# A first strip of 576 tokens, and one batch's attention output made by token

## The chip, the cores and the metric

The kernel runs on one core of one Trainium2 chip. The metric is the device time of one execution in microseconds (us). The kernel before takes 312.56 us, the median of 3 runs (312.52 to 312.74). Smaller is better.

## The reference

Linear attention without a softmax, an RMS norm over each head's output, and a bilinear feed-forward layer, over 8 batches of 576 tokens (4608 tokens in all), 8 heads of 64:

```python
kv = np.einsum('bhsd,bhse->bhde', k, v)
out = np.einsum('bhsd,bhde->bhse', q, kv)
rms = np.sqrt(np.mean(out * out, axis=-1, keepdims=True) + 1e-06)
x = (out / rms * g_norm)          # then (b, s, h*d): 4608 x 512
a = x @ w_a                        # 512 -> 1536
b = x @ w_b
return (a * b @ w_out)             # 1536 -> 512
```

The inputs are float32; the kernel works in bfloat16 with float32 sums.

## The kernel before

**The feed-forward layer.** The 4608 tokens are cut into nine strips of 512 (`STRIP`). `xt` holds x transposed (features on the partitions, tokens along the row). For each strip, twelve units (`Unit`, called by `ffn_ab`, one for each 128 of the 1536 hidden features) make a and b: four matmuls with a weight block of `wa_t` (`part_a`), which ScalarE copies to SBUF, then four with `wb_t` (`part_b`), which VectorE multiplies by that copy into `abt`. Then four groups of 128 tokens (`ffn_o`, `o_mm`, `o_out`) multiply `abt` with `wo_t`: twelve matmuls each, a copy out of PSUM by VectorE or ScalarE in turn, and a store on SyncE's DMA queue (SP). Every one of these is a "product" (`product`, L159): a 128x128 weight block against 512 columns. While `halves[0]` is set, a product is issued as two matmuls of 64 weight columns each.

**Attention.** A batch has four pairs of heads. Its x can be made in two ways.
- By channel (batches 0 and 1): `qtr` transposes q on TensorE, `kv1` makes k'v, then x, the squares, their sums by a product with `ones` (`pss`, L227), the reciprocal root (L233) and the scaling into `xt` (`pst`, L240). Batch 1 uses `x` with the block-diagonal `kvb`.
- By token (batches 2 to 7): q is cast to bfloat16 into a DRAM tile `qs` by two GpSimd DMAs and transposed into `qT` by one DMA transpose on SP (`transpose_q`, L153). k and v are loaded into `ktl` and `vtl` by four GpSimd DMAs. `load_late` (L136) issues all six; its first instruction, the copy `gate`, holds GpSimd until the previous batch's `qT` has landed. `kv` (L170) makes k'v, `tx` (L286) x in five chunks c of 128 tokens (the last of 64 new ones), `tsq` squares on ScalarE, `tss` sums on VectorE, `trs` takes the root on ScalarE and multiplies by the gain on GpSimd (L330), and `txt` (L336) scales on VectorE into `x_tok` and issues a DMA transpose into `xt` on SP (L343).

**Order.** Every engine takes its instructions in the order in which the program writes them; there is no scheduler. Strip 0 runs on batch 0's x. Then strip 0's four groups of `ffn_o` are cut in `pieces` (L574), and between them stands batch 1's attention by channel. Then strips 1 to 7 run, and strip s has beside it the attention of batch s + 1: `slot(A, s, n)` (L601) is called after unit n, and once in the middle of it with n - 0.5, and a table says at which n stand `kv` (k0) and `tx` (x0) and how far after x0 each of the other steps stands. n = 12 to 15 are the strip's four groups of `ffn_o`. `load_late` and `transpose_q` of later batches stand at fixed n as well (L644 to L649).

**DMA queues.** GpSimd's queue brings, in this order: batch 0, the weights `wa_t` and `wb_t` in six column blocks of 256 (`load_ab`), the twelve rows of `wo_t`, batch 1's q, k and v, and then batch 2 (`load_late(2)`). SP's queue takes the stores and all DMA transposes, in program order: each waits there for what it reads.

Of the kernel before, what the change touches and what calls it, by code (L numbers as in the profile page):

```python
# [15 lines left out]
def kernel(  # L16
# [11 lines left out]
    nc = tc.nc  # L28
# [14 lines left out]
    EARLY = 2  # L43
    KORD = tuple(range(KC))

    pool = ctx.enter_context(tc.tile_pool(name="sb", bufs=1))
    psum = ctx.enter_context(tc.tile_pool(name="ps", bufs=1, space=bass.MemoryType.PSUM))

# [17 lines left out]

    qT = [sb([128, NP, S], BF16, f"qT{i}") for i in range(2)]
    kvs = [sb([128, NP, D], BF16, f"kvs{i}") for i in range(2)]

    kvb = sb([128, NP, 128], BF16, "kvb")  # L70
    xt = sb([128, KC, n_tok], BF16, "xt")
    abt = [[sb([128, STRIP], BF16, f"ab{i}_{f}") for f in range(FC)] for i in range(2)]
    a_sb = [sb([128, STRIP], BF16, f"asb{i}") for i in range(4)]
    sq = [sb([128, 2, HF], BF16, f"sq{i}") for i in range(3)]
    rs = [sb([128, 2, HF], FP32, f"rs{i}") for i in range(3)]
# [58 lines left out]
        nc.gpsimd.dma_start(out=wo_t[:, i, :], in_=wo_v[:, i, :])  # L134

    def load_late(b):  # L136
        if b > EARLY:

            nc.gpsimd.tensor_copy(gate, qT[(b - 1) % 2][0:1, 0, 0:1])  # L139
        d = qs_d[b].rearrange("t (h d) -> t h d", h=H)  # L140
        for hs in (slice(0, NP), slice(NP, H)):
            nc.gpsimd.dma_start(out=d[:, hs, :], in_=q[b, hs].rearrange("h t d -> t h d"))  # L142
        n = 128 * LC
        for t, src in ((ktl[b % 2], k), (vtl[b % 2], v)):
            nc.gpsimd.dma_start(  # L145
                out=t[:, :, 0:LC, :],
                in_=src[b, :, 0:n].rearrange("h (t c) d -> t h c d", c=LC),
            )
            nc.gpsimd.dma_start(
                out=t[0 : S - n, :, LC, :], in_=src[b, :, n:].rearrange("h t d -> t h d")  # L150
            )
# [12 lines left out]
    class Attn:  # L164
# [5 lines left out]
        def kv(self, p, o):  # L170
# [5 lines left out]
            for c, n in enumerate(rows):  # L176
                for j in range(2):
# [4 lines left out]
                        start=(c == 0),  # L182
                        stop=(c == len(rows) - 1),
                    )

        def kv_out(self, ps, src):
            for j in range(2):
                r = slice(j * D, (j + 1) * D)
                nc.scalar.copy(kvb[r, ps, r], src[r])


        def kv1(self, p, i):
# [57 lines left out]
                )  # L250


        def x(self, p, i0):
            for h in range(2):
                product(
                    P[:, i0 + h, 0:HF],
                    kvb[:, p, :],
                    self.qT[:, p, h * HF : (h + 1) * HF],
                    start=True,
                    stop=True,  # L260
                )

        def rows(self, c):
            t0 = min(c * 128, S - 128)
# [19 lines left out]
        def tx(self, lent):  # L286
            self.lent = lent
            for c in range(LC + 1):
                t0, _ = self.rows(c)
                for p in range(NP):  # L290
                    for j, (i, c0) in enumerate(self.place(c)):
                        r = slice(j * D, (j + 1) * D)
                        nc.tensor.matmul(  # L293
                            P[:, i, c0 + p * D : c0 + (p + 1) * D],
                            lhsT=self.qT[r, p, t0 : t0 + 128],
                            rhs=self.kvs[r, p, :],
                            start=True,
                            stop=True,
                        )


            _, r = self.rows(LC)
            for j, (i, _) in enumerate(self.place(LC)):
                nc.scalar.copy(
                    x_last[r, j], P[r, i, 0 : STRIP // 2].rearrange("t (p d) -> t p d", p=NP)
                )

        def tsq(self, c):
            _, r = self.rows(c)
# [7 lines left out]
                axis=mybir.AxisListType.X,  # L317
            )

        def trs(self, c):  # L320
            _, r = self.rows(c)
            n = r.stop - r.start
            nc.scalar.activation(  # L323
                rst[c % 3][r],
                sst[c % 3][r],
                AF.Abs_reciprocal_sqrt,
                bias=eps_t[r],
                scale=1.0 / D,
            )
            nc.gpsimd.tensor_mul(  # L330
                sqt[c % 3][r].rearrange("t j p d -> t (j p) d"),
                rst[c % 3][r].unsqueeze(2).to_broadcast([n, H, D]),
                g_all[r].unsqueeze(1).to_broadcast([n, H, D]),
            )
# [13 lines left out]
    class Unit:  # L348
        n = 0

        def __init__(self, s, fc, a, b):
            self.s, self.fc, self.a, self.b = s, fc, P[:, a, :], P[:, b, :]
            self.t = a_sb[Unit.n % 4]
            Unit.n += 1

        def mm(self, w, kcs):
            t0 = self.s * STRIP
            for kc in kcs:
                product(
                    self.a if w is wa_t else self.b,  # L360
                    w[:, kc, self.fc * 128 : (self.fc + 1) * 128],
                    xt[:, kc, t0 : t0 + STRIP],
                    start=(kc == KORD[0]),
                    stop=(kc == KORD[-1]),
                )
# [2 lines left out]
            self.mm(wa_t, kcs)  # L368
            self.mm(wb_t, kcs)

        def part_a(self, kcs=KORD):
            self.mm(wa_t, kcs)
            nc.scalar.copy(self.t, self.a)  # L373

        def part_b(self, kcs=KORD):
            self.mm(wb_t, kcs)
            nc.vector.tensor_mul(abt[self.s % 2][self.fc], self.b, self.t)  # L377

        def rest(self, kcs=KORD):
            self.part_a(kcs)  # L380
            self.part_b(kcs)

    ab_banks = [4, 1, 2, 0]

# [4 lines left out]
    def ffn_ab(s, fc, between=None):  # L389
        u = Unit(s, fc, ab_bank(), 0)  # L390
        u.part_a()
        if between:
            between()
        u.b = P[:, ab_bank(), :]
        u.part_b()

    def store(t0, t, e0, e1, eng=nc.sync):
# [14 lines left out]
    n_o = [0]  # L412

    def o_mm(s, g, i, fcs, e0=0, e1=d_model):
        for fc in fcs:
            product(
                P[:, i, e0:e1],
                abt[s % 2][fc][:, g * 128 : (g + 1) * 128],
                wo_t[:, fc, e0:e1],
                start=(fc == 0),  # L420
                stop=(fc == FC - 1),
            )
# [41 lines left out]
    make_identity(nc, ident, nomemset=True)  # L464
    nc.scalar.activation(warm, eps_t, AF.Abs_reciprocal_sqrt)
    nc.vector.memset(ones, 0.0)
    nc.vector.memset(kvb, 0.0)
    for t in ktl + vtl:
        nc.vector.memset(t[S - 128 * LC :, :, LC, :], 0.0)
    nc.vector.memset(ones[0:D, 0:D], 1.0 / D)  # L470
# [4 lines left out]
    for c in range(0, KC, 2):  # L475
        for w, src in ((wa_t, wa_v), (wb_t, wb_v)):
            nc.gpsimd.dma_start(out=w[:, c : c + 2, 0:WC], in_=src[:, c : c + 2, 0:WC])  # L477
    for i in range(1, d_ff // WC):
        load_ab(i * WC, (i + 1) * WC)
    for i in range(FC):  # L480
        load_o(i)
    for p in range(NP):
        load_pair(1, p)
    load_late(2)

    X, SS = (4, 0), 6

# [65 lines left out]
    u1.part_a((3,))  # L553
    u0.part_b((2, 3))
    u1.part_b((2, 3))

    u2 = Unit(0, 2, 0, 1)
    u3 = Unit(0, 3, 2, 0)
# [1 line left out]
    u3.part_a()  # L560
    u2.part_b()
    u3.part_b()
    for fc in range(4, FC):
        ffn_ab(0, fc)


    A = Attn(1)
    h1, h2 = range(0, FC // 2), range(FC // 2, FC)

    nc.sync.dma_start(out=gate_d, in_=vt[1][0:1, H - 1, EC - 1, D - 1 : D])  # L570
    nc.sync.dma_start(out=g_all, in_=g_norm.partition_broadcast(128))
    transpose_q(2)
    ffn_o(0, 0, X[0])
    pieces = [(1, h1), (1, h2), (2, h1), (2, h2), (3, h1), (3, h2)]  # L574
    for n, (g, fcs) in enumerate(pieces):

        halves[0] = n > 0
        o_mm(0, g, O, fcs)
        if fcs is h2:
            o_out(0, g, O)  # L580
        if 0 <= n - 2 < NP:
            A.pss(n - 2, SS)
            A.pst(n - 2, X[n % 2])
        if 0 <= n - 1 < NP:
            A.x(n - 1, X[(n - 1) % 2])
            A.psq(n - 1, X[(n - 1) % 2])
        if n < NP:
            A.qtr(n, 2)
            A.kv1(n, 2)
            A.kv_out(n, P[:, 2, STRIP - D :])  # L590
            A.qtr_out(n, 2)
    u0 = Unit(1, 0, 2, 3)
    u1 = Unit(1, 1, 4, 5)
    u0.first((0, 1, 2))
    u1.first((0, 1, 2))
    u0.rest((3,))
    u1.rest((3,))
    ab_banks[:] = [0, 1, 2]


    def slot(A, s, n):  # L601

        kb = P[:, 7, :].rearrange("q (b p e) -> q b p e", b=2, e=D)
        if s == 1:
            k0, xs = 5, (6.5, 8, 9.5, 11, 12.5)
        else:
            k0, x0 = {2: (2, 3.5), 3: (4, 5.5), 4: (0, 1.5), 5: (4, 5.5), 6: (0, 1.5)}[s]
            xs = tuple(x0 + x for x in (0, 1.5, 2.5, 4, 5))

        k0, x0 = {1: (5, 6.5), 2: (1, 2.5), 3: (4, 5.5), 4: (0, 0.5), 5: (4, 5.5), 6: (0, 0.5)}[s]  # L610
        if n == k0 and s in (1, 2, 3, 5):
            halves[0] = s < 5
            two = [A] if s < 3 else [A, Attn(s + 2)]
# [5 lines left out]
        m = n - x0  # L619
        if m == 0:  # L620
            A.tx(ab_bank())
        for c in range(LC + 1):
            if m == 1.5 * c:
                A.tsq(c)
            if m == (1, 2, 4, 5, 7)[c]:
                A.tss(c)
            if m == (1, 2, 4, 5, 7)[c] + 0.5:
                A.trs(c)
            if m == (1, 2, 4, 5, 7)[c] + 1.5:
                A.txt(c)  # L630

    for s in range(1, N_STRIP - 1):
        b = s + 1
        A = Attn(b) if b < B else None
        for n in range(FC + 4):
# [4 lines left out]
                ffn_ab(s, n, amid)  # L640
            if A:
                slot(A, s, n)

            if s == 1 and n == 3:  # L644
                load_late(3)
            if b + 1 < B and n == (12, 4, 8, 5, 8)[s - 1]:
                transpose_q(b + 1)
            if b + 2 < B and n == (14, 10, 14, 8)[s - 1]:
                load_late(b + 2)  # L649
    last = N_STRIP - 1  # L650
    for fc in range(FC):
        ffn_ab(last, fc)
# [44 lines left out]
```

## Time and profile before

| what | us |
|---|---|
| median of 3 runs | 312.56 |
| the profiled execution | 312.61 |
| its span in the trace | 310.8 |
| TensorE busy (share of the span) | 304.3 (98%) |
| VectorE, ScalarE, GpSimd busy | 140.6, 117.0, 101.3 |
| first unit of strip 0 starts | 14.10 |
| strip 0's `ffn_o` and batch 1's attention | 35.15 to 49.96 |
| strip 1's units | 49.96 to 72.39 |
| strip 1's `ffn_o` | 72.39 to 82.75 |

Times of stages are counted from the start of the span, which lies about 1.8 us inside the execution's own time. The granted TensorE clock is 1.00 of full speed over the whole span. The 16 DMA engines are busy for 80% or more of each fortieth of the span up to about 124 us, and for little of it after 195 us.

### The profile page before, as it was taken

The page shows a single profiled execution, that of the slowest core. Times are in us where ns is not written, and L with a number is a line of the kernel's source. Part 1 is how long each engine was busy: PE and PEld are TensorE (multiplying, and loading weights), DVE is VectorE, ACT ScalarE, POOL GpSimd, SP SyncE. Part 2 cuts the span into 40 slices and gives each one's busy share as a digit, 9 for nine tenths or more (in the row PEclk, how much of TensorE's full clock was granted, in tenths as well). Part 3 has the DMA queues.
Part 4 walks back from the last instruction along what each step waited for, and adds up shares of the span by engine and source line. Part 5 has one row for each costly group of instructions (what it writes and reads, how often), then busy time and mean ns, then how long its engine had stood idle before and what let it go on. Part 6 is the DMA issues. An engine that isn't in the chain of part 4 may idle for free.

```text
span 310.8 us, 6542 instructions
## 1 busy us (share of the span) xinstructions
PE 304.3 (98%) x2684; PEld 157.6 (51%) x2701; DVE 140.6 (45%) x235; ACT 117.0 (38%) x231; POOL 101.3 (33%) x123
## 2 busy tenths in 40 slices
PE   7899999999999999999999999999999999999996
PEld 3444476655555555555555555444444444444444
DVE  4544335458248603484386123752782143214321
ACT  3743255354255313551564034632651233123310
POOL 8954991093274630043646300221240000000000
PEclk9999999999999999999999999999999999999999
DMA  8999999999899999047998990073021200030002
GB/s 180 197 196 199 201 188 168 161 169 184 174 137 185 139 174 193 2 84 134 178 177 118 162 188 2 19 160 110 20 51 42 103 1 0 34 103 0 0 36 101
DMA packets 94403, 36.29 MB, mean 117 GB/s; under 512 B 64934, under 2 KB 89894, under 8 KB 94374
## 3 DMA queue, kind: packets, MB, share of 16 engines
q0 software_dynamic: 59120, 18.44, 56.6%
q1 hardware_dynamic: 34786, 16.93, 25.0%
q10 hardware_dynamic: 468, 0.51, 0.6%
q8 instruction: 21, 0.34, 0.5%
q14 instruction: 8, 0.07, 0.1%
HBM read 37.78 MB, written 12.98 MB: 163 GB/s over the span
## 4 chain that ended last, share of the span: by engine, by line
PE 79%; DMA 12%; POOL 7%; issue 1%; ACT 0%; POOLq 0%
PE P L161 77%; DMA wb_t<-in_moe_w_b_dram 6%; DMA vtl<-in_v_dram 4%; DMA wo_t<-in_moe_w_out_dram 2%; PE P L293 1%; PE P L178 1%; POOL vt L119 1%; POOL qt L119 1%; POOL qs L142 1%; POOL kt L119 1%; POOL wa_t L477 0%; POOL wb_t L477 0%; POOL wo_t L134 0%; POOL ktl L145 0%; POOL vtl L145 0%
## 5 line engine op out<-in xcount | busy, mean ns | idle before, releaser
L377 DVE TENSOR_TENSOR ab<-P,asb 128x512 bf16<-128x512 f32 x108 | 74.4, 691 | 103.2 <-PE P L161 99.9
L161 PE MATMUL P<-xt,wb_t 128*64 128x512 bf16 (+1 forms) x641 | 111.4, 379 | 0.2
L161 PE MATMUL P<-xt,wa_t 128*64 128x512 bf16 (+1 forms) x636 | 111.0, 379 | 0.6 <-issue 0.2
L373 ACT CAST asb<-P 128x512 bf16<-128x512 f32 x108 | 63.1, 586 | 89.6 <-PE P L161 89.5
L161 PE MATMUL P<-wo_t,ab 128*64 128x512 bf16 (+3 forms) x673 | 95.5, 371 | 0.3
L161 PEld LDWEIGHTS <-ab 128*64 128x64 bf16 (+1 forms) x678 | 47.5, 106 | 45.0
L161 PEld LDWEIGHTS <-wa_t 128*64 128x64 bf16 (+1 forms) x644 | 46.0, 106 | 46.2 <-issue 0.6
L161 PEld LDWEIGHTS <-wb_t 128*64 128x64 bf16 (+1 forms) x644 | 45.8, 106 | 45.8
L330 POOL TENSOR_TENSOR sqt<-rst,g_all 128x512 f32<-128x512 f32 (+1 forms) x24 | 25.0, 1046 | 83.0 <-ACT rst L323 83.0
L429 ACT COPY osb<-P 128x512 f32<-128x512 f32 x17 | 10.0, 586 | 70.2 <-PE P L161 60.2
L431 DVE COPY osb<-P 128x512 f32<-128x512 f32 x18 | 12.4, 691 | 44.9 <-PE P L161 40.4
L142 POOL DMA_DIRECT2D qs<-in_q_dram x12 | 19.8, 1654 | 0.7 <-issue 0.3
L314 DVE TENSOR_REDUCE sst<-sqt 128x8 f32<-128x512 f32 (+1 forms) x24 | 16.3, 680 | 1.7 <-ACT sqt L310 1.5
L339 DVE TENSOR_TENSOR qv<-P,sqt 128x512 bf16<-128x512 f32 x18 | 12.3, 681 | 0.0
L330 POOL TENSOR_TENSOR k_x<-rst,g_all 128x512 f32<-128x512 f32 x6 | 6.3, 1044 | 17.4 <-ACT rst L323 17.4
L323 ACT ACTIVATE rst<-sst,eps_t 128x8 f32<-128x8 f32 (+1 forms) x30 | 9.0, 300 | 7.2 <-DVE sst L314 7.0
L310 ACT ACTIVATE sqt<-P 128x512 f32<-128x512 f32 x18 | 10.5, 585 | 0.1
L243 DVE SCALAR_TENSOR_TENSOR xt<-P,g_col,rs 128x288 bf16<-128x288 f32 x16 | 7.5, 511 | 5.1 <-ACT rs L233 5.1
L134 POOL DMA_DIRECT2D wo_t<-in_moe_w_out_dram x12 | 6.4, 530 | 6.7 <-DMA wb_t<-in_moe_w_b_dram 3.2
L233 ACT ACTIVATE rs<-P,eps_t 128x576 f32<-128x576 f32 (+1 forms) x9 | 6.1, 689 | 3.7 <-PE P L161 3.4
L139 POOL COPY gate<-qT 1x1 bf16<-1x1 bf16 x5 | 0.9, 177 | 18.9 <-DVE kvs L618 14.0
L444 PE MATMUL P<-zeros 128*128 128x512 bf16 x16 | 5.8, 510 | 1.2 <-DVE eps_t L461 1.2
(72 smaller groups left out, 131.7 us busy)
## 6 DMA issues: line engine op xcount, KB each, us to landing
out_dram<-osb SPq DMA_DIRECT2D x23, 256.0 KB, 2.1
qs<-in_q_dram POOLq DMA_DIRECT2D x12, 288.0 KB, 7.5
ktl<-in_k_dram POOLq DMA_DIRECT2D x6, 512.0 KB, 9.6
vtl<-in_v_dram POOLq DMA_DIRECT2D x6, 512.0 KB, 12.2
out_dram<-osb SPq DMA_DIRECT2D x13, 128.0 KB, 2.4
wo_t<-in_moe_w_out_dram POOLq DMA_DIRECT2D x12, 128.0 KB, 6.0
wa_t<-in_moe_w_a_dram POOLq DMA_DIRECT2D x5, 256.0 KB, 8.9
wb_t<-in_moe_w_b_dram POOLq DMA_DIRECT2D x5, 256.0 KB, 9.5
```

The lines of the kernel that those rows point to most:

```text
L119: nc.gpsimd.dma_start(out=t[:, hs, :, :], in_=src[b, hs].rearrange("h (t c) d -> t h c d", c=EC))
L142: nc.gpsimd.dma_start(out=d[:, hs, :], in_=q[b, hs].rearrange("h t d -> t h d"))
L161: nc.tensor.matmul(o[r], lhsT=lhsT[:, r], rhs=rhs, **kw)
L310: nc.scalar.activation(sqt[c % 3][r], self.by_head(c)[r], AF.Square)
L314: nc.vector.reduce_sum(sst[c % 3][r], sqt[c % 3][r].rearrange("t j p d -> t (j p) d"), axis=mybir.AxisListType.X,)
L323: nc.scalar.activation(rst[c % 3][r], sst[c % 3][r], AF.Abs_reciprocal_sqrt, bias=eps_t[r], scale=1.0 / D,)
L330: nc.gpsimd.tensor_mul(sqt[c % 3][r].rearrange("t j p d -> t (j p) d"), rst[c % 3][r].unsqueeze(2).to_broadcast([n, H, D]), g_all[r].unsqu ...
L339: nc.vector.tensor_mul(t[r].rearrange("t (p j) d -> t j p d", j=2), self.by_head(c)[r], sqt[c % 3][r])
L373: nc.scalar.copy(self.t, self.a)
L377: nc.vector.tensor_mul(abt[self.s % 2][self.fc], self.b, self.t)
L429: nc.scalar.copy(t, P[:, i, :])
L431: nc.vector.tensor_copy(t, P[:, i, :])
```

## The change

- **Strip 0 has 576 tokens in its units**, all of batch 0. The units of strip 0 take 448 columns (`CUT`); a new `ffn_end(fc, i)` makes the last 128 columns for two units at once, in one PSUM bank: 16 products of 128 columns, one copy on ScalarE, two multiplications on VectorE. Strip 1's units take the other 448 of the first 1024 columns. `abt` is one tile of 1024 columns for each fc. `ffn_o` keeps its groups of 128 tokens.
- **Batch 1's x is made by token.** Its `qtr` and `kv1` (`pair(p)`) stand behind the units 5, 8, 10 and 11 of strip 0; `x`, `kv_out`, `kvb`, and for this batch `psq`, `pss` and `pst`, are gone. `tx` and its chain stand behind strip 0's last `ffn_end`, beside strip 0's `ffn_o`, whose first three groups run side by side, one fc after the other. The chunk 4 of this batch is written out in strip 1 (n = 4). Strip 1's first two units take their first 256 columns before the other 192.
- **Loads.** Batch 1's q, k and v stand between the column blocks of `wa_t` and `wb_t`, and `wo_t` behind them. `load_late(2)` has a gate of its own: it waits for VectorE's write of batch 1's chunk 3.
- **Later slots.** In strip 1, `kv` of batch 2 moves from n = 5 to 9 and `tx` from 6.5 to 10, and the five chunks are written out at n = 12.5, 13, 14, 15 and, in strip 2, n = 1. In strip 2, `kv` of batch 3 moves from 1 to 3 and `tx` from 2.5 to 4.5; in strip 3, `kv` from 4 to 5 and `tx` from 5.5 to 6.5.
- **`transpose_q` and `load_late`** stand: batch 2's transpose at strip 1, n = 3; `load_late(3)` at strip 1, n = 6; batch 3's transpose at strip 2, n = 0; `load_late(4)` at strip 2, n = 3; batch 4's transpose at strip 2, n = 4; `load_late(5)` at strip 2, n = 12.

```diff
+    def ffn_end(fc, i):
+        n = S - CUT
+        t = a_sb[Unit.n % 4][:, 0 : 2 * n]
+        Unit.n += 1
+        for m, w in enumerate((wa_t, wb_t)):
+            for j in range(2):
+                for kc in KORD:
+                    product(
+                        P[:, i, (2 * m + j) * n : (2 * m + j + 1) * n],
+                        w[:, kc, (fc + j) * 128 : (fc + j + 1) * 128],
+                        xt[:, kc, CUT:S],
...
+        nc.scalar.copy(t, P[:, i, 0 : 2 * n])
+        for j in range(2):
+            nc.vector.tensor_mul(
...
-    for i in range(1, d_ff // WC):
-        load_ab(i * WC, (i + 1) * WC)
+    load_ab(WC, 2 * WC)
+    load_ab(2 * WC, 3 * WC)
+    load_pair(1, 0)
+    load_ab(3 * WC, 4 * WC)
...
+    load_heads(1, qt[1], q, hs[1])
+    load_heads(1, kt[1], k, hs[1])
+    load_ab(4 * WC, 5 * WC)
+    load_heads(1, vt[1], v, hs[1])
+    load_heads(1, qt[1], q, hs[2])
+    load_ab(5 * WC, 6 * WC)
+    load_heads(1, kt[1], k, hs[2])
+    load_heads(1, vt[1], v, hs[2])
+    load_pair(1, 3)
     for i in range(FC):
         load_o(i)
-    for p in range(NP):
-        load_pair(1, p)
-    load_late(2)
...
+    ffn_end(0, 6)
...
+    ffn_end(2, 7)
...
     for fc in range(4, FC):
+        if fc == 9:
+            ab_banks.remove(4)
         ffn_ab(0, fc)
...
-        if 0 <= n - 2 < NP:
-            A.pss(n - 2, SS)
-            A.pst(n - 2, X[n % 2])
-        if 0 <= n - 1 < NP:
-            A.x(n - 1, X[(n - 1) % 2])
-            A.psq(n - 1, X[(n - 1) % 2])
...
+        if fc in (5, 8, 10, 11):
+
+            halves[0] = True
+            pair((5, 8, 10, 11).index(fc))
+        if fc % 2:
+            ffn_end(fc - 1, (ab_banks[0] if fc == FC - 1 else 6 + fc // 2 % 2))
+
+
+    lent = ab_banks[1]
+    A.tx(lent)
+    A.tsq(0)
+    A.last_out(0)
+    A.tsq(1)
+    A.tss(0)
+    A.trs(0)
...
+    A.txt(3)
...
+    nc.gpsimd.tensor_copy(gate, x_tok[1][0:1, 0, 0, 0:1])
+    load_late_q(2)
+    load_late_kv(2)
+    A.tg(4, nc.gpsimd)
+
+    three = (ab_banks[2], ab_banks[0], ab_banks[1])
+    for fc in range(FC + 2):
+        for g, i in enumerate(three):
+            f = fc - (0, 0, 2)[g]
+            if 0 <= f < FC:
+                o_mm(0, g, i, (f,))
+                if f == FC - 1:
+                    o_out(0, g, i)
+    ffn_o(0, 3)
...
-        k0, x0 = {1: (5, 6.5), 2: (1, 2.5), 3: (4, 5.5), 4: (0, 0.5), 5: (4, 5.5), 6: (0, 0.5)}[s]
+        k0, x0 = {1: (9, 10), 2: (3, 4.5), 3: (5, 6.5), 4: (0, 0.5), 5: (4, 5.5), 6: (0, 0.5)}[s]
...
+        if s == 1:
+            sqs, sums = (0, 1, 2, 3, 4), (1, 2, 3, 4, 5)
+            rss, outs = (1.5, 2.5, 3.5, 4.5, 5), (2.5, 3, 4, 5, None)
...
-            if s == 1 and n == 3:
-                load_late(3)
-            if b + 1 < B and n == (12, 4, 8, 5, 8)[s - 1]:
-                transpose_q(b + 1)
-            if b + 2 < B and n == (14, 10, 14, 8)[s - 1]:
-                load_late(b + 2)
+            if s == 1:
+                if n == 3:
+                    transpose_q(2)
+                elif n == 4:
+
+                    Attn(1).txt(LC)
+                elif n == 6:
+                    load_late(3)
+            elif s == 2:
+                if n == 0:
+                    transpose_q(3)
+                elif n == 1:
+                    Attn(2).txt(LC)
+                elif n == 3:
+                    load_late(4)
+                elif n == 4:
+                    transpose_q(4)
+                elif n == 12:
+                    load_late(5)
```

## The prediction

> **What bounds the kernel now.** I read the page's busy shares first, then the timeline of TensorE (PE), then the waits of the DMA transposes and of GpSimd (POOL).
>
> ```profile
> PE 304.3 (98%) x2684; PEld 157.6 (51%) x2701; DVE 140.6 (45%) x235; ACT 117.0 (38%) x231; POOL 101.3 (33%) x123
> PEclk9999999999999999999999999999999999999999
> DMA  8999999999899999047998990073021200030002
> ```
>
> TensorE idles 6.5 us of 310.8, nearly all before 14 us and behind the last matmul. So every matmul that goes is a gain, and every gap that comes is a loss, one for one. The DMA row: the first 16 slices (124 us) leave the queues hardly any room; that is the stretch in which the change moves loads.
>
> TensorE's timeline; columns: start, length, engine, line, operation, count:
>
> ```profile
> 14.10 0.38 PE L161 MATMUL P<-xt,wa_t 128*128 128x512 bf16 x1 [0.16 <-issue]
> 35.15 1.03 PE L161 MATMUL P<-wo_t,ab 128*128 128x512 bf16 x4
> 49.96 0.41 PE L161 MATMUL P<-xt,wa_t 128*64 128x512 bf16 x2
> 71.53 1.03 PE L161 MATMUL P<-xt,wb_t 128*64 128x512 bf16 x8
> 72.39 10.53 PE L161 MATMUL P<-wo_t,ab 128*64 128x512 bf16 x96
> 82.75 1.03 PE L161 MATMUL P<-xt,wa_t 128*64 128x512 bf16 x8
> ```
>
> The landmarks are strip 0 at 14.10, its `ffn_o` at 35.15, strip 1 at 49.96, its `ffn_o` at 72.39, strip 2 at 82.75. From 72.39 to 82.75 there are 48 products: 0.2158 us each, as halves too.
>
> Now two views of the DMA transposes into `xt` (L343). The first is the stretch 70 to 73 us, with `load_late(3)` in flight; the second is 200 to 235 us, where no load runs:
>
> ```profile
> L343 SPq DMA_TRANSPOSE xt<-qv x2: 1223/1230/1236, 70.6 to 72.3; - x2
> DMA to landing us min/median/max: 6.8/7.0/7.2
> ```
> ```profile
> L343 SPq DMA_TRANSPOSE xt<-qv x10: 1171/1195/1227, 199.6 to 233.3; - x10
> DMA to landing us min/median/max: 2.3/2.4/2.5
> ```
>
> The same transpose lands in 2.4 us on quiet queues and in 7 us beside a load. Batch 2's `qT` (issued at 50.5, beside `ktl` and `vtl`) took 11.2 us, against 4.6 us at 201 us. Last, the load itself:
>
> ```profile
> 61.91 0.18 POOL L139 COPY gate<-qT 1x1 bf16<-1x1 bf16 x1 [13.99 <-DVE kvs L618]
> 62.39 3.26 POOL L142 DMA_DIRECT2D qs<-in_q_dram  x2 [0.30 <-issue]
> 68.07 0.72 POOL L149 DMA_DIRECT2D vtl<-in_v_dram  x1
> ```
>
> Its last piece, issued at 68.07, took 10.8 us to land (the view of tile `vtl`): a load is over 17.0 us after its gate here, and 18.9 us after for the next (84.53 to 103.4). The second half of `qs` landed 6.8 us after its issue at 64.0, which is 8.9 us after the gate.
>
> [...]
>
> **Part by part: TensorE's work.**
> Strip 0's units: 96 products of 448 columns at 0.189 are 18.15 us, where 96 of 512 were 20.7. Six `ffn_end` of 16 products of 128 columns: [...] the trace's last 36 products (12 of 256 and 24 of 128 in 2.83 us) leave about 55 ns as well: 5.4 us. [...] I take 5.4. Strip 1's units: 80 products of 448 and 16 each of 256 and 192, 18.2 us. Sum 41.75 against 41.4: plus 0.35.
>
> Batch 1 before: 49.96 - 35.15 less 48 products (10.35) is 4.46 us. It consists of 4 × 0.45 for `qtr` and `kv1`, 4 × 0.48 for `x` and `pss`, and waits, among them 0.4 for the loads of pairs 0 and 1. After: 4 × 0.45, `tx` 0.69 (40 matmuls, as at 63.91), and a wait of about 0.3: the second group of `ffn_o` takes the bank of the last `ffn_end`, which one copy (about 0.38) and two multiplications (0.29 each) must leave first, while only `tx` and one product lie before it. Together 2.8: minus 1.65. Batch 2's `kv` and `tx`, 1.63 us between 59.7 and 65 with a wait for `vtl`, fall to 1.35.
>
> If nothing waits, the landmarks become: strip 0 ends at 39.7, `tx` at 40.4, strip 1 starts at 51.05, its `ffn_o` at 70.6, strip 2 at 80.95. That is 1.8 us before 82.75.
>
> **The loads in strip 0.** Their amount is the same; only the order changes, so `wo_t` rather than batch 1 lands last, at 46.2 (batch 1's last v landed then: SP's wait for `vt` ended at 46.23). At 0.76 us for a 144 KB piece and 1.34 for a 256 KB one (the pace at which GpSimd's ring waits end), `wb_t`'s last block lands at 34.7, needed at 36.0; pair 3's v at 38.5, needed at 38.9; `wo_t`'s rows from 39.2 every 0.67, needed from 40.7 every 0.65. Margins 0.4 to 1.5 us: I charge 0.2.
>
> **The chain of batch 1's x** runs beside `ffn_o`: squares, sum, root, GpSimd 1.04, VectorE 0.68, the chunks overlapped. Chunk 3 needs the buffer of chunk 0, so its write comes 8.2 us after strip 0's end, at 47.9. Chunks 0 and 1 are issued at about 44.3 and 45.8, beside the end of the `wo_t` loads, and are needed at 51; chunks 2 and 3 at 52.8. Hidden, with about 2 us to spare.
>
> **What is late next: batch 2.** Its load begins at 41.3 before and behind chunk 3, at about 48.1, after. With the row of `load_late(3)` (8.9, then 17 to 19 us): `qs` lands at 57, `ktl` and `vtl` at 65 to 67. `kv` stands behind unit 9 of strip 1, at 66.2: a wait of 0 to 1, I take 0.3. The transpose of q starts at 57 with k and v beside it, so 9.6 (batch 4's, at 95.06) to 11.2 us: `qT` at 66.6 to 68.2, and `tx` needs it at 68.4. That just fits.
>
> **The step that decides.** `load_late(3)` is gated by that `qT`: it starts at about 67.4 and is over at 84.4 to 86.3. Batch 2's x is made in just that stretch. The first group of strip 1's `ffn_o` ends at about 73.5; VectorE's order is copy (0.69), sum of chunk 1, chunk 0; so chunk 0's transpose is issued at 75.8, chunk 1's at 78.2. Chunk 2 stands behind the third group's copy on VectorE, and its transpose behind that group's two stores on SP (0.46 each): 1.85 us after that group's end at 78.7, so 80.5. Strip 2's first product needs all three chunks (tokens up to 1535), at 81.5. Beside a load a transpose took 7 us; batch 2's `qT`, issued at 50.5, landed about 1.1 after its load ended. So chunk 2 lands at 85.5 to 87.5; I take 86.4. The gap before strip 2 is 4.9 us, and strip 2 starts 3.65 us later than before. In the kernel before, the same transposes were issued from 70.6 on, with ten us to spare. Bounds: 1.85 + 2.4 after the group's end on quiet queues (a gap of 1.65), and 7.2 after a late issue behind full queues (gap 7).
>
> Two consequences. A gap of 5 us may cost the clock: [...] at an even chance 0.8. And `load_late(5)` now waits for batch 4's `qT` at about 110, is over at 128 to 129.5, and `kv` of batch 5 wants it at about 129: 0 to 1, I take 0.2. Strip 3 onward is as before; GpSimd's and ScalarE's added work lies under TensorE.
>
> **Sum.** 3.65 + 0.8 + 0.2 = 4.65 on the profiled execution's 312.6 (its span of 310.8 and 1.8 around it, 0.05 from the median): 317.2 us.
>
> **The rivals.**
> 1. *The forecast*, 0.60: 314.8 to 319.5.
> 2. *The load has passed*, 0.20. Batch 2's `qT` lands in 4.6 to 6.6 us, as later batches' did, so `load_late(3)` is gated at 62 to 63 and nearly over at 80. Only the line on VectorE and SP stays: minus 1.8, plus 0.5 of waits, plus 1.65: about 313.0, from 312.2 to 314.3. For it: four of the six `qT` transposes. Against it: both that ran beside k and v took 9.6 and 11.2.
> 3. *Faster*, 0.12. If chunk 2 lands within 0.7 us of strip 2's wish, TensorE keeps its 1.8 less 0.5 to 1: 311.2. For it: the sum of TensorE's work is sure to shrink. Against it: a quiet transpose already lands 1.65 late.
> 4. *More waits*, 0.08. The clock falls and the strip-0 loads, with margins of 0.4, come late too: 319.5 to 321.5.
> That the matmuls don't go is no case: they are deleted.
>
> **The numbers.** About 0.2% (0.6 us) is what this measurement can tell from no change. Faster by more: 0.11 of case 3 and 0.02 of case 2, 0.13. Within: 0.10 of case 2 and 0.01 of case 3, 0.11. Slower: 0.76. The likeliest is 317.2, its own range 314.8 to 319.5. Leaving out 0.1 at each side, the range goes from 311.6 to 320.0.
>
> **What would show it.** A hole in TensorE's row at about 81.5 us, ended by a DMA into `xt`; L343's landings near 7 us between 75 and 82; the second `gate` at 67 us; strip 1 starting near 51 and `ffn_o` of strip 1 near 70.6. The forecast is wrong if the gate comes by 63 us, if those transposes land in 3 us, or if strip 0's rows show gaps before `wa_t`, `wb_t` or `vt`.

## The result and the profile after

| | before | after |
|---|---|---|
| median of 4 runs of each, same chip (us) | 312.54 (312.41 to 312.74) | 329.17 (328.09 to 329.69) |
| ratio, 95% interval | 1 | 1.0527 (1.0497 to 1.0557) |
| profiled execution, its span (us) | 312.6, 310.8 | 329.69, 327.6 |
| strip 1's `ffn_o` starts at | 72.39 | 73.75 |
| strip 2 starts at | 82.75 | 92.92 |
| strip 2's `ffn_o` starts at | 104.91 | 117.41 |
| strip 4 starts at | 148.43 | 165.00 |

The change costs 16.6 us. By the landmarks it is lost in three places: 1.4 us before strip 1's `ffn_o`, 11.1 us from there to strip 2's `ffn_o`, 4.1 us in strip 3. Behind the start of strip 4 the two kernels run alike. Executions of one kernel that waits for DMA scatter by 1 to 5 us here, so each trace below stands for its own execution.

The page of the kernel after, busy shares and the rows of 40 slices (8.2 us each):

```profile
PE 309.7 (95%) x2967; PEld 163.9 (50%) x2967; DVE 145.7 (44%) x249; ACT 117.8 (36%) x237; POOL 106.7 (33%) x128
...
PEclk9999999999859999979999999999999999999999
DMA  8999989969979959942499999036212200021002
```

TensorE (PE) was at 98% before and is at 95% now, and its granted clock (PEclk, in tenths of full speed) falls at two places: slices 10 and 11, counted from 0 (82 to 98 us, strip 2's start), and slice 17 (139 to 147 us, strip 3). The waits of TensorE (total, times, longest) name two releasers that had no such row before:

```profile
PE P L167 <- DMA xt<-qv: 8.6, 1, 8.6
PE P L184 <- DMA vtl<-in_v_dram: 3.7, 4, 1.1
```

L167 is the helper of every product, and `xt<-qv` a DMA transpose of x. L184 is `kv`, which waits for a late batch's v. TensorE's timeline (start, length, instruction, count, idle time before it and its releaser) has the places:

```profile
67.87 0.32 PE L184 MATMUL P<-vtl,ktl 128*64 128x64 bf16 x8 [0.75 <-DMA vtl<-in_v_dram]
69.17 0.69 PE L184 MATMUL P<-vtl,ktl 128*64 128x64 bf16 x32 [0.98 <-DMA vtl<-in_v_dram]
...
73.75 10.53 PE L167 MATMUL P<-wo_t,ab 128*64 128x512 bf16 x96
92.92 1.92 PE L167 MATMUL P<-xt,wa_t 128*64 128x512 bf16 x8 [8.64 <-DMA xt<-qv]
94.60 1.95 PE L167 MATMUL P<-xt,wb_t 128*64 128x512 bf16 x8
96.31 1.70 PE L167 MATMUL P<-xt,wa_t 128*64 128x512 bf16 x8
97.82 0.40 PE L167 MATMUL P<-xt,wb_t 128*64 128x512 bf16 x2
```

Strip 1's `ffn_o` ends at 84.28, and nothing runs until 92.92. Each row of `x8` is 4 products in halves. The first three such rows take 1.5 to 1.7 us to the next start, where the kernel before took 0.86 (the granted clock is 0.50 from 88 us to 97). That adds 2.3 us to the gap. Strip 3 shows the same in small, around `kv` of batch 5:

```profile
140.02 0.32 PE L184 MATMUL P<-vtl,ktl 128*64 128x64 bf16 x8 [1.09 <-DMA vtl<-in_v_dram]
141.25 0.70 PE L184 MATMUL P<-vtl,ktl 128*64 128x64 bf16 x32 [0.91 <-DMA vtl<-in_v_dram]
141.75 1.73 PE L167 MATMUL P<-xt,wa_t 128*64 128x512 bf16 x8
143.22 1.97 PE L167 MATMUL P<-xt,wb_t 128*64 128x512 bf16 x8
144.92 1.30 PE L167 MATMUL P<-xt,wa_t 128*64 128x512 bf16 x8
```

Two waits of 2.0 us together, then about 1.7 us lost at half clock (granted 0.50 from 142 us to 145): from 141.75 to batch 4's `tx` at 146.15 it takes 4.40 us, where the kernel before took 2.69 for the same products. Now the cause of the large gap, GpSimd's (POOL's) timeline:

```profile
71.61 0.18 POOL L139 COPY gate<-qT 1x1 bf16<-1x1 bf16 x1 [14.89 <-DMA qT<-qs]
...
77.82 0.72 POOL L155 DMA_DIRECT2D vtl<-in_v_dram  x1
78.52 2.09 POOL L328 TENSOR_TENSOR sqt<-rst,g_all 128x512 f32<-128x512 f32 x2
```

`load_late(3)` begins at 71.61, when batch 2's `qT` has landed, and its issues hold GpSimd until 78.52; only then come the gain multiplications (L328) of batch 2's chunks 0 and 1. The DMA queue of SP, and the landings of the first two of these transposes:

```profile
80.37 1.29 SPq L341 DMA_TRANSPOSE xt<-qv  x1
...
82.86 1.29 SPq L341 DMA_TRANSPOSE xt<-qv  x1
...
85.36 1.23 SPq L341 DMA_TRANSPOSE xt<-qv  x1
```
```profile
L341 SPq DMA_TRANSPOSE xt<-qv x2: 1287/1290/1294, 80.4 to 82.9; - x2
DMA to landing us min/median/max: 7.4/8.2/9.0
```

Chunk 2's transpose, issued at 85.36, frees TensorE at 92.92. The last piece of the load, issued at 77.82, landed 14.6 us later (the view of that line), at 92.4. Chunk 0's transpose, issued at 80.37, had landed at 87.8, well ahead of the load's end, chunk 1's at 91.9. Batch 1's four transposes, at 44.9 to 48.9 with no such load beside them, landed in 2.4 to 2.5 us.

### The profile page after: what moved, and what is told of

The parts are those of the page before. It is cut to its first block, busy times and chain, and to the rows that moved or that the text cites. A ratio compares the mean times of both kernels' runs of the same rounds, so it can differ in the third digit from the quotient of the medians.

```text
span 327.6 us, 7135 instructions
## 1 busy us (share of the span) xinstructions
PE 309.7 (95%) x2967; PEld 163.9 (50%) x2967; DVE 145.7 (44%) x249; ACT 117.8 (36%) x237; POOL 106.7 (33%) x128
## 4 chain that ended last, share of the span: by engine, by line
PE 79%; DMA 12%; POOL 5%; issue 1%; ACT 1%; DVE 1%; SPq 0%; ACTq 0%; DVEq 0%; POOLq 0%
PE P L167 75%; DMA vtl<-in_v_dram 4%; DMA qT<-qs 4%; DMA xt<-qv 2%; POOL qs L146 2%; DMA qv<-in_v_dram 2%; PE P L283 1%; PE P L184 1%; POOL sqt L328 1%; PE P L203 1%; POOL vtl L151 1%; PE P L217 0%; DVE qv L337 0%; POOL ktl L155 0%; DVE sst L305 0%
## 5 line engine op out<-in xcount | busy, mean ns | idle before, releaser
L379 DVE TENSOR_TENSOR ab<-P,asb 128x512 bf16<-128x512 f32 (+1 forms) x108 | 73.0, 676 | 114.1 <-PE P L167 105.8
L167 PE MATMUL P<-xt,wa_t 128*64 128x512 bf16 (+7 forms) x764 | 115.5, 359 | 8.7 <-DMA xt<-qv 8.6
L167 PE MATMUL P<-xt,wb_t 128*64 128x512 bf16 (+7 forms) x764 | 114.5, 357 | 0.0
L375 ACT CAST asb<-P 128x512 bf16<-128x512 f32 (+1 forms) x108 | 61.9, 574 | 97.3 <-PE P L167 97.2
L167 PE MATMUL P<-wo_t,ab 128*64 128x512 bf16 (+3 forms) x696 | 95.0, 372 | 0.0
L167 PEld LDWEIGHTS <-wa_t 128*64 128x64 bf16 (+1 forms) x764 | 50.2, 109 | 53.1 <-issue 11.6
L167 PEld LDWEIGHTS <-wb_t 128*64 128x64 bf16 (+1 forms) x764 | 50.4, 108 | 43.9 <-issue 1.9
L167 PEld LDWEIGHTS <-ab 128*64 128x64 bf16 (+1 forms) x696 | 47.3, 106 | 46.2 <-DVE ab L398 0.3
L328 POOL TENSOR_TENSOR sqt<-rst,g_all 128x512 f32<-128x512 f32 (+1 forms) x27 | 28.1, 1044 | 87.4 <-ACT rst L317 87.4
L305 DVE TENSOR_REDUCE sst<-sqt 128x8 f32<-128x512 f32 (+1 forms) x28 | 19.1, 681 | 2.1 <-ACT sqt L301 1.9
L317 ACT ACTIVATE rst<-sst,eps_t 128x8 f32<-128x8 f32 (+1 forms) x35 | 10.5, 300 | 17.2 <-DVE sst L305 17.0
L328 POOL TENSOR_TENSOR k_x<-rst,g_all 128x512 f32<-128x512 f32 x7 | 7.3, 1042 | 16.7 <-ACT rst L317 16.7
L184 PE MATMUL P<-vtl,ktl 128*64 128x64 bf16 x240 | 5.1, 196 | 3.7 <-DMA vtl<-in_v_dram 3.7
L184 PEld LDWEIGHTS <-ktl 128*64 128x64 bf16 x240 | 4.8, 112 | 5.0 <-issue 4.3
```

The lines of the kernel that those rows point to most:

```text
L167: nc.tensor.matmul(o[r], lhsT=lhsT[:, r], rhs=rhs, **kw)
L184: nc.tensor.matmul(o[j * D : (j + 1) * D, :], lhsT=kk[0:n, 2 * p + j, c, :], rhs=vv[0:n, 2 * p + j, c, :], start=(c == 0), stop=(c == len( ...
L305: nc.vector.reduce_sum(sst[c % 3][r], sqt[c % 3][r].rearrange("t j p d -> t (j p) d"), axis=mybir.AxisListType.X,)
L317: nc.scalar.activation(rst[c % 3][r], sst[c % 3][r], AF.Abs_reciprocal_sqrt, bias=eps_t[r], scale=1.0 / D,)
L328: eng.tensor_mul(sqt[c % 3][r].rearrange("t j p d -> t (j p) d"), rst[c % 3][r].unsqueeze(2).to_broadcast([n, H, D]), g_all[r].unsqueeze(1 ...
L379: nc.vector.tensor_mul(abt[self.fc][:, self.c0 : self.c0 + self.n], self.b, self.t)
```

## The experiments

The theory after the reading: the loss consists of waits on DMA and of the clock behind them. Batch 2's load ends late, so `qT` and with it load 3 come late, and load 3 runs beside batch 2's x. Rivals for the gap: the order on VectorE and SP; GpSimd's queue; the strip of 576 tokens by itself. All times are medians of four executions (five in experiment 7 and for the first kernel of experiment 9, one where said), beside the kernel before on the same chip.

**1. The clock alone.** TensorE is kept busy through the gap with products of zeros that nothing reads:

```diff
     for s in range(1, N_STRIP - 1):
+        if s == 2:
+            dummy(32, O)
```

> The changed kernel with 32 products on zeros put on TensorE between strip 1's last group of ffn_o and strip 2's first unit (32 x 0.216 = 6.9 us, into the bank of the third group). In the changed kernel TensorE stands still there for 8.6 us and strip 2's first units then run at half clock. Theory 'clock' (the gap also costs the clock, about 2.3 us): the zeros fit into the gap, strip 2 still starts near 92.9 us, its first units run at 0.86 us for four products at once, and the time falls by 2 to 2.4 us, to about 327. Rival (the slow first units have another cause, for instance SBUF or the DMA traffic): no change, or slower if the gap was not free.

325.9 us, ratio 1.0424 (1.0407 to 1.0442): 3.3 us less than after. TensorE's timeline:

```profile
87.77 7.08 PE L466 MATMUL P<-zeros 128*128 128x512 bf16 x32
94.78 1.05 PE L167 MATMUL P<-xt,wa_t 128*64 128x512 bf16 x8
```

The first unit runs at full rate at once (0.88 us from its first row to the next), and strip 2's units take 22.2 us instead of 24.5: these are the 2.3 us of the clock. Little of them is in the time, since strip 2 starts 1.9 us later (`kv` of batch 2 waited 3.2 us here, and the zeros ended late). Of the 2.8 us between the two profiled executions 0.45 are won up to strip 2's `ffn_o`; the other 2.35 are from strip 3, whose waits were 1.3 us in this run and cost no clock (the rows behind them started 0.87 us apart). That the time fell by about what was expected is in large part chance.

**2. Load 3 away from batch 2's x.** It is issued behind chunk 3's write:

```diff
-                elif n == 6:
+                elif n == 15:
+                    nc.gpsimd.tensor_copy(gate, x_tok[1][0:1, 0, 0, 0:1])
                     load_late(3)
```

> load_late(3) stands at the end of strip 1 (n = 15) and is gated by VectorE's write of batch 2's chunk 3, so that no load runs beside batch 2's transposes. Theory 'load' (those transposes share the DMA engines with load_late(3)): they land in 2.4 to 3 us, strip 2 starts at about 88 instead of 92.9, the gap before it falls from 8.6 to about 3.5; but batch 3's k and v come about 15 us later, so that its kv in strip 2 waits some 12 us and the whole gets slower, about 334. Rival 'order' (the gap is made by chunk 2's place behind the copy on VectorE and the stores on SP): the gap stays near 8.6 us.

337.69 us, one execution. TensorE's timeline, then the landings of batch 2's x:

```profile
89.12 1.05 PE L167 MATMUL P<-xt,wa_t 128*64 128x512 bf16 x8 [1.73 <-DMA xt<-qv]
...
106.81 0.43 PE L184 MATMUL P<-vtl,ktl 128*64 128x64 bf16 x8 [10.59 <-DMA vtl<-in_v_dram]
```
```profile
L341 SPq DMA_TRANSPOSE xt<-qv x3: 1188/1232/1250, 81.6 to 86.4; - x3
DMA to landing us min/median/max: 2.5/2.5/2.6
```

The same transposes land in 2.5 us and the gap is 1.73: the load makes the rest of it (in experiment 8, with load 3 moved too, they land in the same time). The 1.73 that stays is the line on VectorE and SP with quiet queues. But load 3 is now at 91.6, and its v comes 10.6 us late for `kv` of batch 3.

**3. The order alone.** Chunk 2 goes ahead of VectorE's copy and of the stores:

```diff
-            rss, outs = (1.5, 2.5, 3.5, 4.5, 5), (2.5, 3, 4, 5, None)
+            rss, outs = (1.5, 2.5, 3, 4.5, 5), (2.5, 3, 3.5, 5, None)
```

> In strip 1 chunk 2 of batch 2 is written out at n = 13.5 instead of 14 (its root at 3 instead of 3.5 behind tx), which puts it in front of the third group's copy on VectorE and in front of that group's two stores on SP. Theory 'load': the transpose is issued about 1.2 us earlier but lands with the end of the load at about 91.6; the gap falls by 0 to 1.2 us, the time is 328 to 329. Rival 'order': chunk 2 lands before strip 2 wants it or up to 2 us after; the gap falls below 3 us and the time to about 322 (with the cold clock gone).

328.3 us, 1.0505 (1.0453 to 1.0556), not to be told from after. The gap was 6.98, not below 3; chunks 0 and 1 landed in 7.5 and 7.9 us. In this execution `kv` of batch 5 waited 2.8 us instead of 2.0, again at half rate behind it: the next row took 1.69 us to the following start, where 0.86 is the usual.

**4. Load 2 earlier**, without the gate that holds it behind batch 1's chunk 3:

```diff
-    nc.gpsimd.tensor_copy(gate, x_tok[1][0:1, 0, 0, 0:1])
     load_late_q(2)
```

> The gate in front of load_late(2) is gone: GpSimd issues it right behind its third multiplication of batch 1, at about 46.2 instead of 48.9 us. Theory 'load': the chain load 2, its qT, load 3 comes 2.7 us earlier as a whole; kv's wait in strip 1 goes, the gate of load 3 falls to about 69, strip 2 starts near 90.2, the time falls by about 2.7 us to 326.5, less up to 0.5 if batch 1's last two chunks, now beside a load, come late to strip 1. Rival 'order': the gap before strip 2 keeps its length; only kv's wait (1.7 us) is won. A third possibility: batch 1's transposes beside the load come so late that strip 1 waits and nothing is won.

326.12 us, 1.0399 (1.0347 to 1.0452; the ratio leaves out the longest execution, 328.1 us, and that is the one profiled). TensorE's timeline:

```profile
52.44 0.63 PE L167 MATMUL P<-xt,wa_t 128*64 128x256 bf16 x8 [0.86 <-DMA xt<-qv]
...
57.61 0.52 PE L167 MATMUL P<-xt,wa_t 128*64 128x192 bf16 x8 [3.23 <-DMA xt<-qv]
...
89.50 1.05 PE L167 MATMUL P<-xt,wa_t 128*64 128x512 bf16 x8 [1.76 <-DMA xt<-qv]
...
137.58 0.43 PE L184 MATMUL P<-vtl,ktl 128*64 128x64 bf16 x8 [4.38 <-DMA vtl<-in_v_dram]
```

Load 3's gate comes at 68.5 instead of 71.6, load 3 is over at 83.8, and the gap before strip 2 is back to the 1.76 of quiet queues. Now batch 1's transposes have load 2 beside them, and strip 1 waits 4.1 us for them; and batch 5's `kv` in strip 3 waits 5.2 us in all. The waits are moved, not removed.

**5. `qT` behind the load.** The transpose of batch 2's q waits until v has landed:

```diff
+                    nc.sync.dma_start(out=gate_d, in_=vtl[0][0:1, H - 1, LC, D - 1 : D])
                     transpose_q(2)
```

> On SP, batch 2's qT transpose is held until the last piece of vtl of batch 2 has landed (a one-element DMA that reads it stands in front). In the changed kernel load 2 took 20.2 us from its gate and qT 12 us from its issue, side by side; the prediction had charged 17 to 19 and 9.6 to 11.2. Theory 'side by side' (each slows the other): the load is over 17 us after its gate, at about 66, kv of batch 2 waits not at all or below 0.5 us, qT lands 4.6 to 6.5 us after its issue, at 71 to 72.5, tx waits about 2.5 us, and the gate of load 3 stays at about 71.6. Rival (the load is long for another reason, such as the stores of strip 0 or batch 1's chunks): vtl still lands near 69 and kv waits as before; qT then lands near 74 and everything behind it is 2 to 3 us later.

329.75 us, one execution. Alone, load 2 was over about 18 us after its gate instead of 20.2, and `kv` of batch 2 did not wait. But `qT`, issued at 67.5, came 2.9 us late for `tx`, load 3's gate stood at 72.3 and the gap was 7.4. What one transfer gains by going alone, the other loses.

**6. The late `kv` of strip 3.** Batch 5's `kv` goes from product 5 to product 10 of strip 3. Its result then lies in a bank that still holds part of batch 4's x, so that part of batch 4's x is overwritten in this kernel.

```diff
-            two = [A] if s < 3 else [A, Attn(s + 2)]
+            two = [A] if s < 4 else [A, Attn(s + 2)]
...
+        if s == 3 and n == 10:
+            a = Attn(5)
+            for p in range(NP):
+                a.kv(p, kb[:, 1, p, :])
+            nc.scalar.copy(a.kvs, kb[:, 1])
```

> kv of batch 5 alone is moved from n = 5 to n = 10 of strip 3, 8.6 us later; its x is wanted only in strip 4. In the changed kernel it waited 2.0 us for vtl at 140 us and TensorE's units behind it ran slow for about 1.8 us. Theory 'chain of loads' (load 5 comes late because each load is gated by the qT of the batch before, and the wait costs the clock too): the wait and the slow units go, 3.5 to 4 us less, about 325.4. Rival (the units behind it are slow for another reason): 2 us less.

325.49 us, 1.0418 (1.0395 to 1.044): 3.7 us less than after, which is the waits of 2.0 us and the 1.7 us of half clock behind them. TensorE's timeline, in strip 3 at batch 4's `kv`, which now stands alone:

```profile
138.20 0.80 PE L184 MATMUL P<-vtl,ktl 128*64 128x64 bf16 x40
138.83 1.03 PE L167 MATMUL P<-xt,wa_t 128*64 128x512 bf16 x8
```

Strip 3 reaches its `ffn_o` 23.3 us after its start, where after took 26.9.

**7. The gain multiplication on VectorE**, so that batch 2's chunks 0 to 2 don't stand on GpSimd behind the load's issues:

```diff
-                A.trs(c)
+                A.trs(c, nc.vector if s == 1 and c < 3 else nc.gpsimd)
```

> The changed kernel with the gain multiplication of batch 2's chunks 0 to 2 on VectorE, so that these chunks don't stand on GpSimd behind the issues of the third load (which keep GpSimd until 78.5; chunk 0's multiplication could start at 75.6). Theory 'GpSimd's queue': the transposes are issued 2 to 3 us earlier (chunk 0 near 78, chunk 2 near 83.2), still land in 7 to 8 us, and the gap before strip 2 falls from 8.6 to 6 to 7 us; 326 to 327.5 us. Theory 'the load's end decides': whatever their issue, the transposes come through only as the load ends near 92, so they land later after their issue (9 to 10 us) and the gap stays at 8 to 8.7; 328.5 to 329.7 us.

328.52 us, 1.0535 (1.0517 to 1.0552): no gain in the median of five. The profiled execution was the quickest of the five (324.48; the others took 328.5 to 329.4). In it the transposes are issued 1.8 to 2.2 us earlier, as "GpSimd's queue" has it, land in 8.0 us, and the gap is 6.56; but load 3's gate came 1.5 us earlier too. Neither theory's numbers fit by themselves. Set beside four other kernels that keep load 3 in its place, the traces suggest which end counts:

| | load 3's gate | its last v lands | strip 2 starts |
|---|---|---|---|
| after | 71.61 | 92.4 | 92.92 |
| 3 (order) | 72.13 | 91.3 | 91.78 |
| 5 (`qT` behind) | 72.34 | 91.8 | 92.45 |
| 6 (`kv` later) | 71.93 | 93.1 | 93.71 |
| 7 (gain) | 70.12 | 90.0 | 90.54 |

In all five strip 2 starts 0.5 to 0.7 us behind the end of the load, whenever its transposes were issued (chunk 2 between 83.5 and 86.0). Experiment 1 keeps load 3 in its place too, but there the zeros set strip 2's start. The order in time is seen in five traces; no run tells what holds the last transpose until then. Not every transpose waits for the end: after's chunk 0 landed 4.6 us ahead of it.

**8. The change mended.** Chunk 2 first in every strip, each next load only behind VectorE's write of chunk 2, each batch's `kv` alone and late in its strip (product 9 in strip 1, else 8), the multiplications of chunks 3 and 4 on VectorE (a part of the edit):

```diff
...
+            if n == (14 if s == 1 else 12) and b + 1 < B:
+                nc.gpsimd.tensor_copy(gate, x_tok[0][0:1, 2, 0, 0:1])
+                load_late(b + 1)
```

> The changed kernel with its order mended: chunk 2 of each batch's x ahead of VectorE's copy and the stores, the next load issued only behind chunk 2's transpose, kv of each batch alone and late in its strip (product 8 of a strip of 16), so that no load runs beside the transposes and no kv stands before its v. If the loss is made of the waits and of the clock behind them: the gap before strip 2 is 1 to 1.8 us, kv of batch 2 still waits 2 to 3 us, no other wait is over 0.5 us, and the time is 315 to 317 us. If something else in the change (the strip of 576 tokens itself) costs time: over 319 us although the waits are gone.

320.24 us, 1.0233 (1.0205 to 1.0262): 8.9 us less than after, and 3.2 above the top of what was expected. TensorE's timeline:

```profile
70.12 0.32 PE L184 MATMUL P<-vtl,ktl 128*64 128x64 bf16 x8 [3.08 <-DMA vtl<-in_v_dram]
71.51 1.06 PE L184 MATMUL P<-vtl,ktl 128*64 128x64 bf16 x32 [1.07 <-DMA vtl<-in_v_dram]
72.33 1.73 PE L167 MATMUL P<-xt,wa_t 128*64 128x448 bf16 x8
...
88.67 1.05 PE L167 MATMUL P<-xt,wa_t 128*64 128x512 bf16 x8 [1.07 <-issue]
```

The gap is down to 1.07, and chunks 0 and 1 land in 2.5 and 2.6 us. `kv` of batch 2 now waits 4.15 us, with half rate behind it (the next row of 448 columns took 1.48 us to the following start, where 0.76 is the usual), and three later `kv` wait 0.4 to 0.9 each. In the kernels whose code is that of after up to here (experiments 1 to 3 and 6 to 8), the last v of load 2 freed TensorE between 69.1 and 71.5, so the same code gives a wait of 1.6 to 4.2 us; what makes it vary is open.

**9. The strip of 576 without x by token.** Three kernels keep it and the new order of its loads, make batch 1's x by channel among strip 0's `ffn_o`, and give load 2 and all later steps the old places. The first takes `ffn_o`'s groups one after another:

```diff
+    load_late_q(2)
+    load_late_kv(2)
...
+        if 0 <= n - 1 < NP:
+            A.px(n - 1, X[(n - 1) % 2])
+            A.psq(n - 1, X[(n - 1) % 2])
...
-        k0, x0 = {1: (9, 10), 2: (3, 4.5), 3: (5, 6.5), 4: (0, 0.5), 5: (4, 5.5), 6: (0, 0.5)}[s]
+        k0, x0 = {1: (5, 6.5), 2: (1, 2.5), 3: (4, 5.5), 4: (0, 0.5), 5: (4, 5.5), 6: (0, 0.5)}[s]
```

> The first half of the change alone: strip 0 of 576 tokens with ffn_end, the new order of loads and the pairs' products inside strip 0, but batch 1's x by channel as before (px, squares, sums by product, pst) between strip 0's groups of ffn_o, with load_late(2) right behind wo_t and all later slots, transposes and loads where the kernel before has them. TensorE's work against the kernel before: plus 0.35 for the narrower products, minus 0.4 for the waits on pairs 0 and 1, plus 0.5 where the first units wait for weights. Theory 'by token is what breaks it': no gap before strip 2, no cold clock, 312 to 313.2 us. Rival (the strip of 576 tokens or the order of loads costs by itself): over 315.

319.31 us, 1.0223 (1.0203 to 1.0242), a miss. TensorE's waits:

```profile
PE P L167 <- DMA wo_t<-in_moe_w_out_dram: 1.8, 7, 0.3
```

No `kv` and no strip waits any more. `ffn_o` of strip 0 took 17 us: `wo_t`'s rows, the last of the loads, come every 0.65 us, slower than groups one by one ask for them, and the first group took 6.4 us, where its products need 2.6. The profiled execution is the quickest of the five (317.47), with the clock at 1.00; in the others its mean was 0.988 to 0.995. The second kernel puts three groups side by side, as after does:

> The kernel with the strip of 576 tokens and the new order of its loads, but batch 1's x by channel among strip 0's wo products, with the first three groups of wo side by side, so that its rows are wanted as slowly as they land; later strips as before. If x by token with its long chain (and so the late gate of load 2) is what breaks the change: ffn_o of strip 0 takes 12 to 13 us instead of the 17 of the run before it, strip 2 starts with no gap, and the time is 312 to 314 us. If the strip of 576 and its load order cost time by themselves: over 315 us.

316.83 us, 1.0141 (1.0126 to 1.0156): by its own figures a point for the strip's own cost, and a miss, since `ffn_o` of strip 0 still took 16.7 us where 12 to 13 were expected. The 4.2 us over before stand at strip 1's `ffn_o` (76.58) as at the end, and in strip 0's `ffn_o` lie 1.75 us of waits for banks and operands, and x products for each head, up to 0.66 us a pair, where the kernel before has both heads in one, about 0.25. The third kernel makes them with the block-diagonal `kvb` again and spreads the pairs and groups (a part of the edit, against the second kernel):

```diff
...
-                A.px(p, 4)
+            A.x(px.index(k), 4)
...
```

> The run before, with batch 1's x made as in the kernel before: both heads of a pair in one product of 128 rows (a block-diagonal kv), 0.25 us a pair less overlap instead of 0.66, and the pairs spread so that their banks are free in time. If what is left over the kernel before (4.4 us) is the form of these products and the waits for banks, all of it inside strip 0's ffn_o: 1.6 us for the form and 1 to 1.7 for the waits go, 313.3 to 314.3 us, and strip 2 starts at about 84. If the strip of 576 tokens and its load order cost time by themselves: no less than 316 us.

314.79 us, 1.0075 (1.0058 to 1.0092), half a us over what was expected. TensorE's timeline:

```profile
55.02 0.95 PE L168 MATMUL P<-xt,wa_t 128*64 128x448 bf16 x8
...
74.64 10.53 PE L168 MATMUL P<-wo_t,ab 128*64 128x512 bf16 x96
85.00 1.03 PE L168 MATMUL P<-xt,wa_t 128*64 128x512 bf16 x8
```

Strip 2 follows `ffn_o` without a hole, 2.25 us later than before, and stays so to the end. Strip 1 starts 5.1 us later than before and is 2.8 us shorter, mostly by the columns that moved into strip 0; the rest is lost before strip 1. So the strip with its loads costs at most 2.4 us in this form, and the other 14.2 of after's 16.6 go with x by token and the places of loads and `kv` that belong to it. This last pair of causes was taken back as one; no run parts them. No kernel of this study beats the one before.

## Why the prediction was wrong

Forecast were 317.2 us (range to 320.0) and this very hole: batch 2's x beside load 3. The direction, the place and the releaser held; the size did not, and 329.17 lies outside the range. Four terms make up the 12 us that are missing: the gap (3.7), the later end of strip 1's `ffn_o` (2.8), the clock behind the gap (1.5) and strip 3 (about 3.9).

| step | predicted | measured |
|---|---|---|
| `ffn_o` of strip 1, if nothing waits; with the waits charged | 70.6; 71.1 | 73.75 |
| load 2's gate | 48.1 | 48.88 |
| wait of `kv` of batch 2 | 0.3 | 1.73 |
| load 2 over | 65 to 67 | 69.1 |
| transpose of batch 2's q issued | 57 | 59.44 |
| `qT` of batch 2 landed, gate of load 3 | 67.4 | 71.61 |
| load 3 over | 84.4 to 86.3 | 92.4 |
| chunk 2 issued; strip 2 starts | 80.5; 86.4 | 85.36; 92.92 |
| gap before strip 2 | 4.9 | 8.64 |
| half clock behind it | 0.8 | 2.3 |
| strip 3's `kv`, with its clock | 0.2 | 3.7 (strip 3 in all 4.1) |

**The step that failed** is "it starts at about 67.4 and is over at 84.4 to 86.3". The assumption that hung on it, that the last transpose lands just behind the load's end (1.1 us was taken from batch 2's `qT`), fits the five traces (0.5 to 0.7 us). The end itself was 6 to 8 us later, by four terms of one chain. Load 2's gate was 0.8 us late. Its q took 10.5 us from the gate until it could be transposed, where 8.9 were taken. `qT` took 12 us from its issue at 59.4, where about 10.4 were taken (9.6 to 11.2). Load 3 took 20.8, where 17.0 to 18.9 were taken. These durations had been read off the kernel before, each with the neighbours it had there, and every one of them came out above its upper end, so that the upper ends added along the chain (87.1) would still have fallen short. It was not one unlucky execution: in the five kernels of the table load 3's gate stood at 70.1 to 72.3 and the load took 19.1 to 21.2 us. Experiments 4 and 5 show how the durations move with their neighbours: load 3 took 15.3 us with `x` issued only at its end, load 2 about 18 without `qT` (one execution). The upper bound "gap 7" fell short for the same reason.

**The wish came later too**, 84.28 instead of 81.5, which made the gap smaller than the lateness of the load: 1.4 us more wait of `kv`, about 0.6 more around `kv` and `tx` (`qT` came just late for it), 0.5 in strip 0, where a weight load waited 0.5 us for `wa_t` at about 16.4. The third group's end at 78.7 is a slip of 0.2 us (78.9 by the prediction's own 81.5), which changes nothing.

**The clock** was put at 0.8, an even chance of its price; that was the author's estimate, and the kernel before, whose granted clock is 1.00 throughout, shows no such price. In after TensorE idles from 84.28, and the granted clock is 1.00 up to 87 us, 0.69 on the mean of the next microsecond and 0.50 from 88 on, so it fell some 3.1 us into this gap. It came back at about 97.6 (0.69 on the mean of the microsecond from 97 on, 1.00 from 98), 4.7 us after work began: at half speed that is the 2.3 us lost, 1.5 more than was charged.

**Strip 3** is the term that was missed in kind. "0 to 1, I take 0.2" had priced a wait alone. Batch 5's load ends behind its `kv` because all loads hang in one chain, each gated by the `qT` of the one before; its 2.0 us of waiting then cost the clock as well (granted 0.50 from 142 us to 145), 1.7 us more.

**GpSimd's queue** was not in the prediction: a gate at 67.4 would have had the issues over by 74.3, ahead of chunk 0; at 71.61 they stand before its multiplication, whose root was ready at 75.6, for 2.9 us. In experiments 3 and 7, each alone, this and the order on VectorE and SP mattered little while the load ran to 90 or later.

**What held.** TensorE's deleted work: batch 1's own products, `tx` and the wait behind it came to 2.9 us where 2.8 were counted, and the `ffn_end` of 16 products took 55.6 ns a product, where about 55 were taken; a product of 448 columns took 0.189 us, as charged. Strip 0's loads cost no more than the 0.5 us, where 0.2 were charged. The rival "faster" fell with the first view, and "the load has passed" with the gate at 71.6; its price for quiet queues, a gap of 1.65, is what experiments 2 and 4 measured (1.73 and 1.76). The rival "more waits" had the clock fall too, but put its other waits at strip 0's loads, and its 321.5 was too small as well.

## What to carry to other kernels

Where transfers are chained (load, transpose, gate, next load) on queues that have no room, add their durations along the chain with the neighbours that they will have after the change; a delay of one was paid by the next here (without load 2's gate, load 3's came 3.1 us earlier). A duration read off a trace holds for the neighbours it had there (load 3 took 20.8 us beside batch 2's x, 15.3 where that x was issued only at its end); where the stretch gets fuller, the longest reading is no upper end. In the five traces here the matmul started 0.5 to 0.7 us behind the end of the load, however early its transpose was issued. Price a wait of TensorE with the clock that it may cost: here 8.64 us of waiting cost 2.3 more, and 2.0 us cost 1.7. Before work that needs no transfer (x by channel) is replaced by work that needs four transposes in the busiest stretch, ask which load will then stand beside them.

## What was not expected of the hardware

- The clock fell behind two waits of 1.09 and 0.91 us with 8 small matmuls between them: the granted clock was 0.50 from 142 us to about 145.4. In other runs 2.2 us in all (experiment 5, strip 3; the rows behind took up to 1.70 us, where 0.86 is the usual) and 1.90 us (experiment 6, batch 2's `kv`; 1.48 and 1.57 us, where 0.76 is) had half rate behind them too, while 1.75 us (experiment 7, strip 3; 0.86), 1.34 us (experiment 1, strip 3; 0.87) and even 2.43 us (experiment 3, batch 2's `kv`; 0.76) did not. What sets apart the waits that cost the clock, no run shows.
- A DMA transpose of one chunk lands in 2.4 to 2.6 us where no load is beside it (batch 1 in after, batch 2 in experiment 2). Beside load 3 it took 6.3 to 9.2 us in the five kernels of the table (two chunks of each, as far as the traces show them), and 5.6 and 6.7 in experiment 1. How the load slows it, and why strip 2 came 0.5 to 0.7 us behind the load's end in all five kernels, no run shows.
